# Two AV runs of two head pairs instead of four runs of one, and a full-array last block in the second GEMM

## The chip, the cores and the metric

The kernel runs on one core of a Trainium2 chip. The metric is the device time of the whole kernel in microseconds (us), from its first instruction to its last. Before the change it is 345.63 us, the median of three runs (345.2 to 345.86). The profile that is read below is one execution of its own, with a span of 343.4 us.

A core has five engines with a queue of instructions each: PE (TensorE, the matrix unit), DVE (VectorE), ACT (ScalarE), POOL (GpSimd) and SP (SyncE, which here only starts transfers). They wait for one another by semaphores.

## The reference

Forgetting attention for 8 batches of 8 heads, 576 tokens, head size 64, followed by a two-layer network with an exact GELU on all 4608 tokens:

```python
scores = scale * np.matmul(q, k.transpose(0, 1, 3, 2))
cum = np.cumsum(np.log(np.clip(f, 0.0001, 1.0)), axis=-1)
scores = np.where(causal, -1e9, scores + cum[:, :, :, None] - cum[:, :, None, :])
attn = softmax(scores)
x = np.matmul(attn, v)            # (8, 8, 576, 64), then to (4608, 512)
h = x @ w_in                      # 512 -> 2048
out = gelu(h) @ w_out             # 2048 -> 512
```

The kernel computes it in bfloat16 with sums in float32.

## The kernel before

**Attention.** The eight heads of a batch are four pairs (`i` = 0 to 3). Queries and keys are held transposed, one head of a pair in partitions 0 to 63 and the other in 64 to 127. For each pair, `scores` (L270) computes the causal part of the scores in four tiles (`t` = 0 to 3): keys in partitions, queries along the free axis, both heads side by side. Its matmuls contract over 64 rows, so they use half of the array's rows each, and the two heads run beside one another. The exponential on ACT (L299) brings a tile from PSUM to SBUF, and POOL zeroes what lies above the diagonal (L301). Score tiles live in two PSUM buffers of two banks ("s"), so a third tile can begin only when the exponential of the first is done.

`attend` (L313) multiplies the exponentials with the values, which carry the forgetting weights and a column for the softmax sum (this product is called AV). It is 15 matmuls of the full array, 128x65, for each head, into one PSUM bank; there are two such banks ("o"). `normalize` (L328) then takes the reciprocal of the sums (L333) and multiplies (L334), both on DVE, and writes x.

x must be transposed for the first GEMM. From the third batch on (`b` > 2) a transposing DMA on SP's queue does it for pairs 0 to 2 (`x_dma`, L358), and PE does it for pair 3 (`to_xT`, L346), through an "o" bank. In the batch `b` = 2 PE does it for pairs 2 and 3.

**First GEMM.** `gemm1` (L370) takes the first 512 tokens of the batch in 16 blocks of four full-array 128x512 matmuls, and GELU on ACT brings each block to SBUF. The last 64 tokens of all batches are gathered and done at the end.

**Second GEMM.** It is spread as filler into the attention of the next batch, so that PE has work while ACT computes exponentials. `gemm2_rows` (L446) is a generator of steps: four blocks of 128 tokens (`ts` = 0 to 3), 16 steps each, one for each 128 of the 2048 contracted elements. A step is written as "r" or "n". An "r" step is two half-array matmuls, rows 0 to 63 into one PSUM bank and rows 64 to 127 into another. An "n" step is one full-array matmul into the first bank. DVE copies the second bank out (L474) and adds the first (L476), and the block is stored from SP. A plan names for each block its number, the PSUM pool that it holds ("o", "m" or "s", of which "m" also serves the first GEMM), and its 16 steps. `take(fill, n)` (L521) issues the next n steps.

**The order of the work** is written out by hand; the engines run their instructions in that order. In `attention(b)` (L621), for `b` = 2 to 7, the sixteen score tiles are issued one after another, each followed by as many steps as `FILL` (for `b` = 2, `FILL_2`) says. After tile 1 of pairs 1, 2 and 3 come the two heads of AV of the pair before, and its `x_dma`. The AV of pair 3 follows the last score tile and eight more steps. Then come six steps, the transpose of pair 3, and the remaining steps. The batch `b` = 2 has more filler, `gemm2_third`: 16 full-array steps of `gemm2_half`, 32 steps of `PLAN_0` and 64 of `PLAN_1`.

Of the kernel before, what the change touches and what calls it, by code (L numbers as in the profile page):

```python
# [11 lines left out]
Alu = mybir.AluOpType  # L12
# [6 lines left out]
HP = 4  # L19
# [20 lines left out]
def where(n, m):  # L40

    q = K0[m]
    for t, parts in enumerate(STILES):
        c = 0
        for nn, q0, w in parts:
            if nn == n and q0 <= q and q + P <= q0 + w:
                return t, c + q - q0
            c += w
    raise KeyError((n, m))
# [3 lines left out]
def kernel(  # L53
# [10 lines left out]
    nc = tc.nc  # L64
# [5 lines left out]
    n_ff = d_ff // P  # L70
# [17 lines left out]
    s_psum = ctx.enter_context(tc.tile_pool(name="s_psum", bufs=2, space=PSUM))  # L88
    o_psum = ctx.enter_context(tc.tile_pool(name="o_psum", bufs=2, space=PSUM))
# [24 lines left out]
    def load_v(b, h0=0, h1=H):  # L114
        if b >= B:
            return
        for n in range(NBLK):
            p0 = D if n == NBLK - 1 else 0
            nc.sync.dma_start(
                v_sb[p0:P, h0:h1, n, :],  # L120
                v[b, h0:h1, K0[n] + p0 : K0[n] + P].rearrange("h p d -> p h d"),
            )
# [14 lines left out]
    for t, op, fill in (  # L137
# [7 lines left out]
            fill=fill,  # L145
# [74 lines left out]
    def transpose_dma(b, h0, h1):  # L220

        if b >= B:
            return
        if b not in tq_of:
            tq_of[b] = [
                tq_pool.tile([P, H, JT // 2, PT], BF16, tag="t" + n, name=f"t{n}{b}")
                for n in "qk"
            ]
        for src, dst in zip(qk_of[b], tq_of[b]):
            nc.sync.dma_start_transpose(  # L230
                dst[:, h0:h1].rearrange("d h j p -> d (h j) p"),
                src[:, h0:h1].rearrange("p h c -> p (h c)"),
            )
# [79 lines left out]
    def attend(b, i, h, ms):  # L313
        if (b, i, h) not in o_of:
            o_of[b, i, h] = o_psum.tile([P, NBLK, D + 1], FP32, tag="o", name="o")
        o = o_of[b, i, h]
        for m in ms:
            for n in range(m + 1):
                t, c = where(n, m)
                nc.tensor.matmul(  # L320
                    o[:, m, :],
                    e_of[b, i, t][:, h, c : c + P],
                    vw_of[b][:, 2 * i + h, n, :],
                    start=(n == 0),
                    stop=(n == m),
                )

    def normalize(b, i, h):  # L328
        if (b, i) not in x_of:
            x_of[b, i] = x_pool.tile([P, NBLK, 2, D], BF16, tag="x", name="x")  # L330
        o = o_of[b, i, h]
        r = x_pool.tile([P, NBLK], FP32, tag="r", name="r")
        nc.vector.reciprocal(r, o[:, :, D])  # L333
        nc.vector.tensor_tensor(  # L334
            x_of[b, i][:, :, h, :],
            o[:, :, 0:D],
            r.unsqueeze(2).to_broadcast([P, NBLK, D]),
            Alu.mult,
        )

    def xT(b):
        if b not in xT_of:
            xT_of[b] = xT_pool.tile([P, n_dm, XC], BF16, tag="xT", name="xT")
        return xT_of[b]

    def to_xT(b, i, copy, pool=m_psum, tag="m", ps=None):  # L346
        if ps is None:
            shape = [P, 2, 1024] if pool is s_psum else [P, XC]
            ps = pool.tile(shape, BF16, tag=tag, name="ps_x")
            if pool is s_psum:  # L350
                ps = ps[:, 0, 0:XC]
        for m in range(NBLK):
            nc.tensor.transpose(  # L353
                ps[:, m * P : (m + 1) * P], x_of[b, i][:, m, :, :], ident_bf
            )
        copy(xT(b)[:, i, :], ps)  # L356

    def x_dma(b, i):  # L358
        nc.sync.dma_start_transpose(
            xT(b)[:, i, :].rearrange("d (m p) -> d m p", p=P),  # L360
            x_of[b, i].rearrange("p m h d -> p (m h d)"),
        )

    def x_tail(b):
        nc.gpsimd.tensor_copy(tails[:, :, b * TL : (b + 1) * TL], xT(b)[:, :, XC - TL :])  # L365
# [28 lines left out]
    def gemm2(c):  # L394
# [35 lines left out]

    PLAN = [
        (0, "o", 16 * "r"),
        (1, "m", 6 * "r" + "n" + 8 * "r" + "n"),
        (2, "m", 9 * "r" + "n" + 6 * "r"),
        (3, "s", 7 * "r" + 9 * "n"),
    ]

    PLAN_0 = [(2, "o", 16 * "r"), (3, "m", 14 * "r" + 2 * "n")]
    PLAN_1 = [
        (0, "m", 14 * "r" + 2 * "n"),  # L440
        (1, "m", 14 * "r" + 2 * "n"),
        (2, "m", 14 * "r" + 2 * "n"),
        (3, "s", 8 * "r" + 8 * "n"),
    ]

    def gemm2_rows(c, plan):  # L446

        for ts, held, steps in plan:
            if held == "s":
                both = s_psum.tile([P, 2, d_model], FP32, tag="s", name="ps2")
                banks = [both[:, 0], both[:, 1]]
            else:
                pool = {"o": o_psum, "m": m_psum}[held]
                banks = [
                    pool.tile([P, d_model], FP32, tag=held, name="ps2")
                    for _ in range(2)
                ]  # L460
            ot = o_pool.tile([P, d_model], FP32, tag="ot", name="ot")
            for kt, step in enumerate(steps):
                last = kt == steps.rindex("r")
                for r in range(2 if step == "r" else 1):
                    rows = slice(r * D, (r + 1) * D) if step == "r" else slice(0, P)
                    nc.tensor.matmul(  # L466
                        banks[r],
                        g_of[c][kt][rows, ts * P : (ts + 1) * P],
                        w_out_sb[rows, kt, :],
                        start=kt == (steps.index("r") if r else 0),  # L470
                        stop=last if r else kt == n_ff - 1,
                    )
                if kt == n_ff - 1 if held == "s" else last:
                    nc.vector.tensor_copy(ot, banks[1])  # L474
                if kt == n_ff - 1:
                    nc.vector.tensor_tensor(ot, ot, banks[0], Alu.add)  # L476
                    store(c, ts, ot)
                yield

    def store(c, ts, ot):  # L480
        nc.sync.dma_start(out[c * S + ts * P : c * S + (ts + 1) * P, :], ot)
# [34 lines left out]
    def gemm2_third():  # L516
        yield from gemm2_half(0, 1)
        yield from gemm2_rows(0, PLAN_0)
        yield from gemm2_rows(1, PLAN_1)

    def take(gen, n):  # L521
        for _ in range(n):
            if next(gen, "end") == "end":
                return
# [89 lines left out]

    FILL = [[7, 6, 3, 3], [1, 3, 3, 2], [1, 3, 3, 3], [1, 3, 3, 3], [8]]
    FILL_2 = [[8, 8, 8, 8], [8, 8, 4, 4], [4, 4, 4, 4], [4, 4, 4, 4], [8]]
    FILL_1 = [[0, 0, 0, 0], [0, 0, 0, 0], [2, 2, 2, 2], [2, 2, 2, 2]]

    def attention(b):  # L621


        fill = gemm2_third() if b == 2 else gemm2_rows(b - 1, PLAN)
        counts = FILL_2 if b == 2 else FILL

        def av(i):
            for h in range(2):
                attend(b, i, h, (0, 1, 2, 3, 4))
                normalize(b, i, h)  # L630

        for i in range(HP):
            for t in range(4):
                scores(b, i, t)
                take(fill, counts[i][t])
                if i and t == 1:
                    av(i - 1)
                    if i < HP - 1 or b > 2:
                        x_dma(b, i - 1)
                if t == 1 and i == 0:  # L640
                    load_v(b + 1)
                if b > 2 and t == 0 and i < 2:
                    transpose_dma(b + 1, 4 * i, 4 * i + 4)
                if b == 2 and t == 1 and i == 1:
                    transpose_dma(3, 0, 4)
                    transpose_dma(3, 4, 8)
        take(fill, counts[HP][0])
        if b == 2:
            to_xT(b, HP - 2, nc.vector.tensor_copy, s_psum, "s")
        av(HP - 1)  # L650
        take(fill, 6)
        to_xT(b, HP - 1, nc.vector.tensor_copy, o_psum, "o")
        x_tail(b)
        take(fill, 999)
# [107 lines left out]
```

The softmax here doesn't subtract the row's maximum and nothing guards it: scores larger than these inputs give would overflow.

## Time and profile before

| | value |
|---|---|
| time | 345.63 us (345.2 to 345.86) |
| span of the profile | 343.4 us |
| from one batch to the next, `b` = 3 to 7 | 35.67 us |
| of it attention with the second GEMM (`b` = 4) | 21.77 us |
| of it the first GEMM | 13.9 us |
| one second-GEMM step, "r" or "n" | 0.216 us |
| AV of one head | 0.48 us |
| exponential of a tile of 128x896 | 0.917 us |
| copy and add of a second-GEMM block on DVE | 0.69 us each |

Busy time of PE is the time in which any of its matmuls is in the pipeline; matmuls overlap, so the rate of work is read from the distance of their starts, not from their lengths. In the chain of work that ended last, each piece is followed back to what released it, and a piece of PE there means that PE had nothing to wait for. A few records of matmuls are missing in the trace, which shows as a short gap with no releaser.

### The profile page before, as it was taken

Reading aid. Unit: us, or ns where it says so; the run is one execution under the profiler, and the core shown is the slowest. Engines: PE = TensorE matmul, PEld = TensorE weight load, DVE = VectorE, ACT = ScalarE, POOL = GpSimd, SP = SyncE. Lnnn points to the kernel's source line nnn. Section 1 sums busy time; section 2 is a strip of 40 time slices with the busy share of each in tenths; the row PEclk is TensorE's granted clock in tenths of the full one; section 3 lists DMA queues with packets and bytes.
Section 4 is the critical chain, followed back from the end, with each engine's and each line's share of the span. In section 5 each row is a group of like instructions: output and inputs, shape, how many; then the busy total and the mean of one; then the engine's idle time right before and its main releaser. Section 6 shows DMA issues by size and latency. Waiting matters only on the chain.

```text
span 343.4 us, 7895 instructions
## 1 busy us (share of the span) xinstructions
PE 328.6 (96%) x3182; PEld 174.7 (51%) x3227; DVE 187.0 (54%) x424; ACT 212.3 (62%) x296; POOL 124.2 (36%) x256
## 2 busy tenths in 40 slices
PE   7799999999999999999999999999999999999995
PEld 3574555445554456545654565446544654444443
DVE  5660355933467935796479646974597542020011
ACT  5986786773644787368746874687468755504600
POOL 8390672228328034543445243714261430000000
PEclk9999999999999999999999999999999999999999
DMA  8999999989993999578945896499900230011013
GB/s 117 178 176 194 201 166 153 170 158 148 237 184 102 139 192 188 82 101 165 211 121 73 141 212 139 71 160 198 169 31 2 65 88 31 2 61 61 0 38 87
DMA packets 99924, 43.03 MB, mean 125 GB/s; under 512 B 78704, under 2 KB 95344, under 8 KB 99888
## 3 DMA queue, kind: packets, MB, share of 16 engines
q1 hardware_dynamic: 82592, 28.37, 41.4%
q0 software_dynamic: 16896, 13.63, 27.2%
q8 instruction: 25, 0.41, 0.5%
q10 hardware_dynamic: 400, 0.52, 0.4%
q14 instruction: 11, 0.09, 0.1%
HBM read 36.85 MB, written 9.44 MB: 135 GB/s over the span
## 4 chain that ended last, share of the span: by engine, by line
PE 89%; issue 2%; POOL 2%; DVE 2%; ACT 2%; DMA 2%; POOLq 0%; ACTq 0%; DVEq 0%
PE ps L375 36%; PE ps L466 25%; PE o L320 9%; PE ps L408 8%; PE s L289 7%; PE ps L501 2%; ACT e L299 2%; DMA k<-in_k_dram 2%; PE ps_x L353 1%; DVE x L334 1%; POOL q L107 1%; PE ps_f L206 1%; POOL k L107 1%; DVE r L333 0%; DVE xT L356 0%
## 5 line engine op out<-in xcount | busy, mean ns | idle before, releaser
L392 ACT ACTIVATE g<-ps 128x512 bf16<-128x512 f32 x144 | 85.3, 597 | 81.1 <-PE ps L375 81.1
L299 ACT ACTIVATE e<-s 128x896 bf16<-128x896 f32 (+2 forms) x128 | 101.2, 836 | 28.5 <-PE s L289 26.8
L375 PE MATMUL ps<-xT,w_in_sb 128*128 128x512 bf16 x497 | 111.4, 379 | 0.8
L466 PE MATMUL ps<-w_out_sb,g 64*128 64x512 bf16 (+1 forms) x731 | 103.0, 376 | 0.8 <-issue 0.8
L375 PEld LDWEIGHTS <-w_in_sb 128*128 128x128 bf16 x576 | 56.0, 98 | 67.5 <-issue 1.8
L301 POOL TENSOR_SCALAR_AFFINE_SELECT e<-e 128x256 bf16<-128x256 bf16 (+1 forms) x135 | 49.2, 383 | 98.9 <-ACT e L299 98.6
L466 PEld LDWEIGHTS <-g 64*128 64x128 bf16 (+1 forms) x756 | 41.5, 94 | 40.4 <-issue 11.9
L244 DVE COPY qT<-tq 64x288 bf16<-64x288 bf16 x96 | 48.7, 507 | 1.4
L289 PE MATMUL s<-qT,kT 64*128 64x320 bf16 (+4 forms) x384 | 45.8, 276 | 3.6 <-ACT e L299 2.7
L260 POOL TENSOR_TENSOR vw<-v_sb,wT 128x640 bf16<-128x640 f32 x31 | 39.6, 1278 | 23.5 <-DMA v_sb<-in_v_dram 23.3
L320 PE MATMUL o<-vw,e 128*128 128x65 bf16 x960 | 36.8, 194 | 3.5 <-issue 2.4
L474 DVE COPY ot<-ps 128x512 f32<-128x512 f32 x26 | 17.9, 689 | 37.1 <-PE ps L466 35.2
L320 PEld LDWEIGHTS <-e 128*128 128x128 bf16 x960 | 34.8, 98 | 5.3 <-PE ps_x L353 0.3
L244 DVE COPY kT<-tk 64x288 bf16<-64x288 bf16 x96 | 33.0, 343 | 1.6
L334 DVE TENSOR_TENSOR x<-o,r 128x320 bf16<-128x320 f32 x64 | 31.4, 491 | 2.4 <-DVE r L333 0.2
L417 DVE COPY ot<-ps 128x512 f32<-128x512 f32 (+2 forms) x9 | 5.7, 632 | 48.8 <-PE ps L408 31.9
L289 PEld LDWEIGHTS <-kT 64*128 64x128 bf16 x384 | 19.5, 94 | 23.2 <-issue 9.7
L408 PE MATMUL ps<-w_out_sb,g 128*128 128x512 bf16 (+2 forms) x142 | 27.9, 355 | 0.1
L333 DVE RECIPROCAL r<-o 128x5 f32<-128x5 f32 x64 | 12.1, 189 | 27.6 <-PE o L320 27.5
L408 PEld LDWEIGHTS <-g 128*128 128x128 bf16 x144 | 13.5, 98 | 14.5
L476 DVE TENSOR_TENSOR ot<-ot,ps 128x512 f32<-128x512 f32 x26 | 17.9, 687 | 1.5
L365 POOL COPY tails<-xT 128x256 bf16<-128x256 bf16 x8 | 3.2, 399 | 31.3 <-DVE xT L356 31.3
(64 smaller groups left out, 158.1 us busy)
## 6 DMA issues: line engine op xcount, KB each, us to landing
out_dram<-ot SPq DMA_DIRECT2D x32, 256.0 KB, 2.3
v_sb<-in_v_dram SPq DMA_DIRECT2D x24, 256.0 KB, 5.3
q<-in_q_dram POOLq DMA_DIRECT2D x6, 576.0 KB, 6.1
k<-in_k_dram POOLq DMA_DIRECT2D x6, 576.0 KB, 8.2
v_sb<-in_v_dram SPq DMA_DIRECT2D x22, 128.0 KB, 5.1
w_in_sb<-in_moe_w_in_dram POOLq DMA_DIRECT2D x4, 512.0 KB, 6.7
w_out_sb<-in_moe_w_out_dram POOLq DMA_DIRECT2D x4, 512.0 KB, 8.4
q<-in_q_dram POOLq DMA_DIRECT2D x4, 144.0 KB, 4.6
```

The source lines that it names most:

```text
L244: nc.vector.tensor_copy(rows[:, odd], src[odd * D : (odd + 1) * D, 2 * i + h].rearrange("d j p -> d p j"),)
L260: eng.tensor_tensor(vw_of[b][:, hs, :, 0:D], v_sb[:, hs, :, :], w.unsqueeze(3).to_broadcast([P, 2, NBLK, D]), Alu.mult,)
L289: nc.tensor.matmul(to, *ab, start=half < 0, stop=half == 1 or not masked)
L299: nc.scalar.activation(et[:, :, z:c], st[:, :, z:c], Act.Exp, scale=scale)
L301: nc.gpsimd.affine_select(out=et[:, :, c0 + z : c0 + P], in_=et[:, :, c0 + z : c0 + P], compare_op=Alu.is_ge, fill=0.0, base=z, pattern=[[ ...
L320: nc.tensor.matmul(o[:, m, :], e_of[b, i, t][:, h, c : c + P], vw_of[b][:, 2 * i + h, n, :], start=(n == 0), stop=(n == m),)
L334: nc.vector.tensor_tensor(x_of[b, i][:, :, h, :], o[:, :, 0:D], r.unsqueeze(2).to_broadcast([P, NBLK, D]), Alu.mult,)
L375: nc.tensor.matmul(ps, w_in_sb[:, kt, ffb * P : (ffb + 1) * P], src[:, kt, 0:TC], start=(kt == 0), stop=(kt == n_dm - 1),)
L392: nc.scalar.activation(g_of[c][ffb], ps, Act.Gelu)
L408: nc.tensor.matmul(pss[ts][:, c0:c1], g_of[c][kt][:, ts * P : (ts + 1) * P], w_out_sb[:, kt, c0:c1], start=(kt == 0), stop=(kt == n_ff - 1),)
L466: nc.tensor.matmul(banks[r], g_of[c][kt][rows, ts * P : (ts + 1) * P], w_out_sb[rows, kt, :], start=kt == (steps.index("r") if r else 0), ...
L474: nc.vector.tensor_copy(ot, banks[1])
```

## The change

Four edits belong together, all of them in work of the batches `b` = 2 to 7.

1. AV: the runs after tile 1 of pairs 1 and 3 are dropped. After tile 1 of pair 2 the four heads of pairs 0 and 1 are issued, with one second-GEMM step behind each of the first two. The four heads of pairs 2 and 3 follow the last score tile, with three steps after the second head and one after the third.
2. Plans: the last block (`ts` = 3) is 16 "n" steps, with one copy on DVE in place of a copy and an add. The other blocks become "r" throughout, but for two "n" steps in block 1, which fall between the AV heads. In `PLAN_1` block 1 holds the "o" banks in place of "m".
3. `FILL` and `FILL_2`: the counts are set to the new order, and the eight steps ahead of pair 3's AV are gone.
4. The transposing DMA of pair 0 is issued after the run of pair 2, together with pair 1's; pair 2's comes after its AV in the tail. In `b` = 2 the PE transpose of pair 2 goes through an "o" bank in place of a score buffer and comes after pair 3's AV.

```diff
     PLAN = [
         (0, "o", 16 * "r"),
-        (1, "m", 6 * "r" + "n" + 8 * "r" + "n"),
-        (2, "m", 9 * "r" + "n" + 6 * "r"),
-        (3, "s", 7 * "r" + 9 * "n"),
+        (1, "m", 14 * "r" + 2 * "n"),
+        (2, "m", 16 * "r"),
+        (3, "s", 16 * "n"),
     ]
...
     PLAN_1 = [
-        (0, "m", 14 * "r" + 2 * "n"),
-        (1, "m", 14 * "r" + 2 * "n"),
-        (2, "m", 14 * "r" + 2 * "n"),
-        (3, "s", 8 * "r" + 8 * "n"),
+        (0, "m", 16 * "r"),
+        (1, "o", 16 * "r"),
+        (2, "m", 16 * "r"),
+        (3, "s", 16 * "n"),
     ]
...
-                if kt == n_ff - 1 if held == "s" else last:
+                if last:
                     nc.vector.tensor_copy(ot, banks[1])
                 if kt == n_ff - 1:
-                    nc.vector.tensor_tensor(ot, ot, banks[0], Alu.add)
+                    if "r" in steps:
+                        nc.vector.tensor_tensor(ot, ot, banks[0], Alu.add)
+                    else:
+                        nc.vector.tensor_copy(ot, banks[0])
                     store(c, ts, ot)
...
-    FILL = [[7, 6, 3, 3], [1, 3, 3, 2], [1, 3, 3, 3], [1, 3, 3, 3], [8]]
-    FILL_2 = [[8, 8, 8, 8], [8, 8, 4, 4], [4, 4, 4, 4], [4, 4, 4, 4], [8]]
+    FILL = [[7, 6, 3, 3], [1, 3, 3, 2], [1, 1, 3, 3], [1, 3, 3, 3]]
+    FILL_2 = [[8, 8, 5, 5], [4, 4, 4, 4], [2, 2, 6, 6], [9, 9, 9, 9]]
...
-        def av(i):
-            for h in range(2):
-                attend(b, i, h, (0, 1, 2, 3, 4))
-                normalize(b, i, h)
+        def av(i, h, n=0):
+            attend(b, i, h, (0, 1, 2, 3, 4))
+            normalize(b, i, h)
+            take(fill, n)
...
-                if i and t == 1:
-                    av(i - 1)
-                    if i < HP - 1 or b > 2:
-                        x_dma(b, i - 1)
+                if (i, t) == (2, 1):
+                    av(0, 0, 1)
+                    av(0, 1, 1)
+                    x_dma(b, 0)
+                    av(1, 0)
+                    av(1, 1)
+                    x_dma(b, 1)
...
-        take(fill, counts[HP][0])
+        av(HP - 2, 0)
+        av(HP - 2, 1, 3)
+        if b > 2:
+            x_dma(b, HP - 2)
+        av(HP - 1, 0, 1)
+        av(HP - 1, 1)
         if b == 2:
-            to_xT(b, HP - 2, nc.vector.tensor_copy, s_psum, "s")
-        av(HP - 1)
+            to_xT(b, HP - 2, nc.vector.tensor_copy, o_psum, "o")
         take(fill, 6)
         to_xT(b, HP - 1, nc.vector.tensor_copy, o_psum, "o")
```

More of the change, by code (lines that the diff above doesn't have):

```diff
@@ L462, in gemm2_rows @@
             for kt, step in enumerate(steps):
-                last = kt == steps.rindex("r")
+                last = kt == steps.rfind("r")
                 for r in range(2 if step == "r" else 1):
```

## The prediction

> **What bounds the kernel now.** I read four views in this order: the page for the engine that carries the span, busy time by stretch for the stages, the chain of waits inside one batch for the joints between kinds of matmul, and the timeline for what the other engines do at those joints. The page:
>
> ```profile
> PE 328.6 (96%) x3182; PEld 174.7 (51%) x3227; DVE 187.0 (54%) x424; ACT 212.3 (62%) x296; POOL 124.2 (36%) x256
> PE 89%; issue 2%; POOL 2%; DVE 2%; ACT 2%; DMA 2%; POOLq 0%; ACTq 0%; DVEq 0%
> ```
>
> TensorE (PE) is busy for 96% and is 89% of the chain that ended last. So a change counts by what it does to PE's starts. Next, two stretches of the fifth batch (b = 4): its attention and the first GEMM behind it. The columns are length, then busy us (and instructions) of PE, weight loads, VectorE (DVE), ScalarE (ACT), GpSimd, then clock, DMA share and GB/s.
>
> ```profile
> 155.08:176.85 21.77, 21.12 (x287) 12.59 (x291) 11.88 (x31) 15.73 (x19) 7.29 (x20) 1.00 0.95 179
> 176.85:190.40 13.55, 13.45 (x62) 6.17 (x63) 13.13 (x27) 8.76 (x15) 7.86 (x11) 1.00 0.53 89
> ```
>
> Attention takes 21.77 us and PE leaves little of it idle; ACT has 6 us free and DVE 10, so they can only hurt in places. GEMM 1 is PE back to back and the change does not touch it. The chain inside this attention (start, us, what):
>
> ```profile
> 159.88 0.36 PE L289 MATMUL s<-qT,kT 64*128 64x256 bf16 x4
> ...
> 160.45 0.60 PE L466 MATMUL ps<-w_out_sb,g 64*128 64x512 bf16 x4
> 161.21 1.11 PE L320 MATMUL o<-vw,e 128*128 128x65 bf16 x30 [0.16 <-issue]
> 162.25 0.36 PE L289 MATMUL s<-qT,kT 64*128 64x448 bf16 x2
> ...
> 164.28 0.34 PE L289 MATMUL s<-qT,kT 64*128 64x64 bf16 x4
> ```
> ```profile
> 164.28 0.34 PE s L289 x4
> 164.62 0.43 PE ps L466 x4
> 165.05 0.16 issue
> 165.21 1.11 PE o L320 x30
> 166.32 0.29 PE s L289 x2
> ...
> 171.57 2.16 PE ps L466 x20
> 173.73 0.16 issue
> 173.89 1.11 PE o L320 x30
> ```
>
> The first block is the PE timeline, the second the chain. An AV run is 30 full-array matmuls; it stands between half-array (64-row) score and GEMM 2 matmuls. One GEMM 2 step is 0.216 us, whether it is "r" or "n" (20 matmuls, 10 "r" steps, in 2.16). The "0.16 issue" hides one "n" step whose record is missing. Price of a joint: the last "r" before the first AV starts at 160.67 (end 161.05, one lasts 0.376); AV starts at 161.21, 0.54 later, of which "r" and "n" are 0.43. So 64 to 128 rows costs **0.10 us**. Back: the last AV matmul starts at 162.13, the score tile at 162.25; 0.13 less 0.032 (AV spacing, 30 in 0.95) again leaves **0.10 us**. 164.28 with 0.34 us is a score tile that waited 0.17 us for ACT to free its PSUM buffer.
>
> What DVE does just ahead of the last AV:
>
> ```profile
> 172.26 0.69 DVE L474 COPY ot<-ps 128x512 f32<-128x512 f32 x1 [0.86 <-PE ps L466]
> 172.99 0.69 DVE L476 TENSOR_TENSOR ot<-ot,ps 128x512 f32<-128x512 f32 x1
> 174.56 0.20 DVE L333 RECIPROCAL r<-o 128x5 f32<-128x5 f32 x1 [0.89 <-PE o L320]
> ```
>
> The third token block's copy and add (1.41 us) are over at 173.68, before the normalisation wants DVE: eight fill steps stand between. The first batch shows AV heads without such steps:
>
> ```profile
> 22.34 0.49 DVE x L334
> 22.83 0.11 DVE r L333
> 22.95 0.03 issue
> 22.98 0.63 PE o L320 x15
> ```
>
> There are two "o" banks, so head n waits for the normalisation of head n-2. Here PE starts 0.146 us after that multiply ends at 22.836; the plain DVE to PE waits elsewhere take 0.055.
>
> **What the Trainium skill says.** "TensorEngine Tiling (Array Packing)", section Key Properties: changing the tiling mode drains TensorE. The trace agrees: 0.10 us each way. "TensorE: Matmul & The Clock Gate", section Architectural detail: only weight loads are pulled ahead, and VectorE and ScalarE are strict FIFO. The trace agrees: a waiting score tile holds all matmuls behind it, and the first batch's normalisation stands behind a copy issued earlier. "PSUM — Partial Sum Buffer", section Terms: a matmul output lies in one bank, and two engines on one bank at once is an error, so an AV run cannot start in a bank that DVE reads. "Perfetto Trace Analysis", section Identifying Dependency Chains: several waits of one instruction can become separate instructions ahead of it; this is such a place in the trace (the 0.146 us) and is my upper price.
>
> **The change part by part (one batch, b = 3 to 7).** I lay the new order against the times of b = 4, queue by queue, with the durations above: exp 0.917, 0.806, 0.917, 0.70 us for the four tiles, back-to-back exps overlapping by 0.1; exp end to next score 0.05; score start to exp 0.40 to 0.49; one AV head 0.476; normalisation 0.72 (0.19 + 0.49 + gaps), 0.63 when queued behind another. The same working on the old order puts GEMM 1 at 176.80 (trace 176.85) and finds its waits: 0.02 and 0.19 at two score tiles (trace 0.015, 0.17), and 0.12 at a GEMM 2 bank (trace 0.17).
>
> *Removed: mode changes.* Old: AV after pairs 0, 1, 2 (six), into the tail, back to scores: 8. New: in and out once, tail, back: 4. Gain 4 x 0.10 = **-0.40**. Steps (64), scores and AV are as many as before.
>
> *Less PE work between scores.* From (1,1) to (2,1) the old order has AV of pair 0 (1.15 us with its switches) to let ACT catch up. The new one has six tiles with 11 steps in a row; ACT needs 3.34 us for four tiles, PE only about 3.3. Tile (1,2) is ready at 161.10 but exp (1,0) ends 161.27: 0.22. Then (2,0) waits 0.12 and (2,1), with one step before it, 0.19. After the AV run, AV of pair 2 is missing behind (3,1): tile (3,2) is ready at 169.47, exp (3,0) ends 169.64: 0.22. Sum **+0.75**; the old 0.19 goes.
>
> *Four heads in a row.* AV (0,0) starts at 163.93. DVE's queue: copy of block 1 (to 164.73), normalise (0,0) (to 165.37), (0,1) (to 165.99), add of block 1 (to 166.68), then pair 1. AV (1,0) is ready at 165.32 and starts at 165.42; (1,1) is ready at 165.90 and starts at 166.05: **+0.26**. Block 2 then finds its bank free: the old bank wait (0.17) goes.
>
> *The tail.* The last "r" of block 2 now stands directly ahead of AV of pair 2: step at 171.10, AV (2,0) 171.41, (2,1) 171.89, three "n" to 173.01. DVE: copy 171.52 to 172.21, add to 172.93, normalise (2,0) only then, to 173.56, since it was issued behind them; (2,1) to 174.19. AV (3,0) needs the bank of (2,0): 173.62 instead of 173.01, **+0.61**. AV (3,1) is ready after one more step at 174.31, its bank at 174.25: no wait. Queued behind it: all of the tail and GEMM 1. Normalise (3,1) ends at 175.65 and the transposes come at 176.1: hidden behind six "n".
>
> *Moved DMA.* The transposing DMA of pair 2 goes from 172.1 to 174.3, when its x is written, behind block 2's store on SP's queue; issue 1.24 us, landing 2.6 to 2.8 us after its start (largest of all 4.9): 177.0. GEMM 1's third matmul wants it at 178.1: free. Those of pairs 0 and 1 start when SP is done with loads (168.1 either way). *Last block all "n":* same 0.216 a step, one DVE op of 0.69 fewer, beside GEMM 1: nothing.
>
> Sum: +0.75 +0.26 +0.61 -0.40 -0.35 (old waits) = **+0.87**. With 0.146 instead of 0.055 at two of the bank waits +1.05. I take 0.95: five batches **+4.75**.
>
> *Batch 2* has 15 switches inside and 7 after: -0.80, and 0.09 of an old wait goes. It has steps in plenty (four to nine a tile), so no exp waits. Bank waits as above, 0.26 and 0.61, plus the transposes of pair 2, which now take an "o" bank instead of a score buffer and wait for normalise (3,0): 0.23. Net +0.2 to +0.5; I take **+0.3**.
>
> Total +5.05. The profiled span of 343.4 would become 348.4; the timed runs (345.2 to 345.86) stand 2.2 above the span, and I keep that: 345.63 + 5.05 = **350.7**.
>
> **Rivals.** *Faster: the switch is dearer than its gap shows*, for instance because loads run late for several steps behind it. Place: 28 removed switches (5 x 4 + 8). New waits less old ones are 5 x 1.27 + 1.0 = 7.4 us, so it decides from 0.26 us a switch; at 0.36 the time is about 343. Against it: step spacing behind every AV is 0.216 from the second step on. *Half of it:* the tail's normalisation does not hold AV (3,0), if the wait there is shorter than queue order makes it. Then 6 x 0.61 falls away: 347.0. Against it: DVE runs in program order throughout. *Late transpose:* pair 2's DMA takes the 4.9 us seen at worst, 1.05 us beyond its slack, in five batches: 355.9. For it: only 3.8 us now lie between its start and its reader, and a store goes ahead of it. Against it: pair 2's landed in 2.6 us in this batch, with the same store behind it.
>
> **How the numbers follow.** Likeliest 0.77 (349.5 to 352.2), half 0.10, late transpose 0.06, faster 0.07. The range 346.9 to 352.6 holds the first two cases less their tails. Runs of before spread by 0.2%, so that is what can be told from no change: faster 0.08, same 0.03, slower 0.89, the "same" being the lower tail of the half case.
>
> **What would show it.** AV runs of 60 and two AV stretches a batch; PE waiting for DVE's multiply ahead of AV (3,0) by about 0.6 us and of (1,0), (1,1) by 0.1 to 0.2; score tiles (1,2), (2,0), (2,1), (3,2) waiting for exp, 0.1 to 0.2 each; attention of 22.7 us instead of 21.8, GEMM 1 unchanged at 13.9 (176.85 to the next score tile at 190.75). Wrong if those AV heads start without idle time, if the batch period falls below 35.66, or if GEMM 1's third matmul waits for a DMA.

## The result and the profile after

The changed kernel takes 351.08 us (median of four runs, 350.52 to 351.89) against 345.75 for the kernel before in the same comparison: a ratio of 1.0155, with a 95% interval of 1.0126 to 1.0183. It is slower by 5.3 us; 350.7 was forecast. The profiled span went from 343.4 to 349.1 us, 5.6 more. Single executions lie 2 to 4 us above their kernel's median, most of them with a lower granted clock (the kernel before once took 350.07 us at a clock of 0.993, against a median of 345.87), so medians are compared here.

The page of the changed kernel, busy time and the chain of work that ended last:

```profile
PE 335.4 (96%) x3195; PEld 175.0 (50%) x3195; DVE 183.4 (53%) x418; ACT 210.6 (60%) x296; POOL 124.7 (36%) x256
PE 64%; DMA 10%; SPq 7%; DVE 6%; ACT 5%; POOL 4%; issue 2%; ACTq 0%; POOLq 0%; DVEq 0%
```

PE is busy for the same share of a longer span. What changed is the chain: PE fell from 89% to 64% of it, and DVE and ACT, 2% each before, now hold 11% together. (DMA and SP have a large share because the chain leaves PE in batch 2 and goes back through a late transfer, of which more below; a share of the chain is not a loss of the same size.) The two stretches of the fifth batch, attention and first GEMM, in the same columns as before:

```profile
156.45:179.14 22.69, 22.02 (x284) 12.65 (x284) 11.59 (x30) 15.41 (x19) 7.76 (x22) 1.00 0.89 165
179.14:193.05 13.91, 13.91 (x65) 6.14 (x64) 13.25 (x28) 8.96 (x15) 7.39 (x10) 1.00 0.62 101
```

Attention has grown from 21.76 to 22.70 us, in all five batches alike; the first GEMM is as long as it was. The chain in that attention (start, us, what; pieces under 0.05 us are left out) shows where:

```profile
161.40 0.21 PE s L289 x4
161.72 0.93 ACT e L299
162.68 0.37 PE s L289 x2
...
165.39 0.62 DVE ot L474
166.00 0.19 DVE r L333
166.21 0.49 DVE x L334
166.71 0.16 DVE r L333
166.87 1.21 PE o L320 x30
...
172.93 0.70 DVE ot L474
173.65 0.69 DVE ot L477
174.34 0.12 DVE r L333
174.48 0.49 DVE x L334
174.97 0.11 DVE r L333
175.12 0.63 PE o L320 x15
```

Read from the top: a score tile (1,2) starts only when an exponential on ACT ends; the second half of the merged AV run starts behind block 1's copy and a normalisation; and in the tail the third AV head starts behind block 2's copy, its add and a normalisation, one after another on DVE. (The last DVE piece ahead of each AV is the reciprocal of the head after; what frees the bank is the multiply before it. It ends at 166.71 and 174.97, and both times PE starts 0.146 us later, with a wait instruction of its own, of 0.05 us, in PE's queue: the same as in the first batch.) A piece of PE in the chain can hide a short wait: the last two heads of the merged run take 1.21 us there because the fourth waits 0.11 us. The timeline of PE across the tail says what that costs:

```profile
172.82 1.12 PE L320 MATMUL o<-vw,e 128*128 128x65 bf16 x30
173.78 0.81 PE L466 MATMUL ps<-w_out_sb,g 128*128 128x512 bf16 x3
175.12 0.63 PE L320 MATMUL o<-vw,e 128*128 128x65 bf16 x15 [0.52 <-DVE r L333]
175.59 0.38 PE L466 MATMUL ps<-w_out_sb,g 128*128 128x512 bf16 x1
```

The three full-array steps start at 173.78, so AV head (3,0) could start 3 x 0.216 later, at 174.43. It starts at 175.12: 0.69 us are lost. (The bracket says 0.52 because it counts from the end of the last step's matmul, which stays in the pipeline for 0.38 us, and not from when the next matmul could have been started.)

The changed kernel's times in batch 4, by the starts of PE's instructions, against the forecast: score tiles (1,2), (2,0), (2,1), (3,2) waited 0.22, 0.09, 0.17, 0.22 us (0.22, 0.12, 0.19, 0.22); AV heads (1,0) and (1,1) 0.18 and 0.11 (0.10 and 0.16); AV head (3,0) 0.69 (0.61, and 0.70 at the upper price). Together 1.68 us. Less four mode changes (0.40) and the old waits (0.35) this is 0.93 us a batch; the batch grew by 0.94.

The span's other parts: batch 2's attention took 33.47 us instead of 33.00 (+0.47), the start before batch 2 came out 0.05 shorter, and in the last batch this stretch of the chain appears:

```profile
285.45 4.38 DMA xT<-x
289.82 0.04 issue
289.87 13.54 PE ps L375 x62
```

The transposing DMA of pair 2 took 4.4 us to land, and the first GEMM's third matmul waited 0.47 us for it. The sum is 5 x 0.94 + 0.47 + 0.47 - 0.05 = 5.6, the whole difference of the spans.

### The profile page after: what moved, and what is told of

It reads as the page before. It is cut to its first block, busy times and chain, and to the rows that moved or that the text cites. A ratio compares the mean times of both kernels' runs of the same rounds, so it can differ in the third digit from the quotient of the medians.

```text
span 349.1 us, 7871 instructions
## 1 busy us (share of the span) xinstructions
PE 335.4 (96%) x3195; PEld 175.0 (50%) x3195; DVE 183.4 (53%) x418; ACT 210.6 (60%) x296; POOL 124.7 (36%) x256
## 4 chain that ended last, share of the span: by engine, by line
PE 64%; DMA 10%; SPq 7%; DVE 6%; ACT 5%; POOL 4%; issue 2%; ACTq 0%; POOLq 0%; DVEq 0%
PE ps L375 31%; PE ps L466 14%; PE ps L408 8%; PE s L289 5%; ACT e L299 4%; DMA v_sb<-in_v_dram 4%; PE o L320 4%; SPq L119 3%; DMA k<-in_k_dram 3%; SPq L230 3%; DMA xT<-x 2%; DVE x L334 2%; DVE ot L474 2%; POOL vw L260 1%; POOL q L107 1%
## 5 line engine op out<-in xcount | busy, mean ns | idle before, releaser
L299 ACT ACTIVATE e<-s 128x896 bf16<-128x896 f32 (+2 forms) x128 | 99.5, 838 | 26.8 <-PE s L289 24.3
L375 PE MATMUL ps<-xT,w_in_sb 128*128 128x512 bf16 x512 | 112.7, 379 | 0.3 <-DMA xT<-x 0.3
L466 PE MATMUL ps<-w_out_sb,g 64*128 64x512 bf16 (+1 forms) x724 | 110.6, 376 | 0.0
L466 PEld LDWEIGHTS <-g 64*128 64x128 bf16 (+1 forms) x724 | 40.5, 95 | 29.2
L244 DVE COPY qT<-tq 64x288 bf16<-64x288 bf16 x96 | 49.6, 517 | 1.5
L289 PE MATMUL s<-qT,kT 64*128 64x320 bf16 (+4 forms) x384 | 44.1, 276 | 4.0 <-ACT e L299 2.7
L474 DVE COPY ot<-ps 128x512 f32<-128x512 f32 x20 | 13.8, 691 | 60.3 <-PE ps L466 60.3
L320 PE MATMUL o<-vw,e 128*128 128x65 bf16 x960 | 39.5, 194 | 3.5 <-DVE r L333 3.1
L289 PEld LDWEIGHTS <-kT 64*128 64x128 bf16 x384 | 20.3, 94 | 28.3 <-issue 13.6
L375 PE MATMUL ps<-tails,w_in_sb 128*128 128x512 bf16 x64 | 14.3, 377 | 0.0
```

Source lines behind the costliest of these rows:

```text
L244: nc.vector.tensor_copy(rows[:, odd], src[odd * D : (odd + 1) * D, 2 * i + h].rearrange("d j p -> d p j"),)
L289: nc.tensor.matmul(to, *ab, start=half < 0, stop=half == 1 or not masked)
L299: nc.scalar.activation(et[:, :, z:c], st[:, :, z:c], Act.Exp, scale=scale)
L320: nc.tensor.matmul(o[:, m, :], e_of[b, i, t][:, h, c : c + P], vw_of[b][:, 2 * i + h, n, :], start=(n == 0), stop=(n == m),)
L375: nc.tensor.matmul(ps, w_in_sb[:, kt, ffb * P : (ffb + 1) * P], src[:, kt, 0:TC], start=(kt == 0), stop=(kt == n_dm - 1),)
L466: nc.tensor.matmul(banks[r], g_of[c][kt][rows, ts * P : (ts + 1) * P], w_out_sb[rows, kt, :], start=kt == (steps.index("r") if r else 0), ...
```

## The experiments

The theory is the prediction's: a mode change costs 0.10 us, and the merged runs pay more than they save, because score tiles come to wait for ACT and AV heads for DVE. The rivals are that the mode change costs something else, that the full-array last block carries the loss, that PE's waits are not for what the trace names, and that the late transpose is the cause.

### What a mode change costs

```diff
 (kernel before)
-        (3, "s", 7 * "r" + 9 * "n"),
+        (3, "s", "rnrnrnr" + 9 * "n"),
```

> The kernel before with three of the seven half-array steps of the last block (rnrnrnr and then nine n), so that PE changes between 64 and 128 rows six times more in each of five batches; the work is the same. Own theory (a switch costs 0.10 us): 30 x 0.10 = 3.0 us slower than before, about 348.7. Rival (a switch costs 0.26 us or more and the change loses elsewhere): 7.8 us slower or more, above 353. If switches are free: no change.

Measured: 348.94 us against 345.87, a ratio of 1.0087 (1.0063 to 1.0112): 3.07 us for 30 mode changes, **0.102 us each**. Every attention of batches 3 to 7 grew from 21.76 to 22.40 us, 0.64 for six. The gap read off the trace was the whole price. The rival that needed 0.26 us falls, and with it the idea that the 28 switches which the change takes away could be worth more than 28 x 0.102 = 2.9 us.

### The full-array last block alone

```diff
 (kernel before)
-        (3, "s", 7 * "r" + 9 * "n"),
+        (3, "s", 16 * "n"),
 # and one copy in place of copy and add for a block without "r"
```

> The kernel before with its last block of batches 3 to 7 as 16 full-array steps and one copy, AV runs left where they were. The number of mode changes stays the same, a step costs 0.216 us either way, and the DVE operation saved lies beside the first GEMM. Own theory: no change (within 0.7 us). Rival (the full-array block itself carries the loss): about 5 us slower.

Measured: 345.91 us against 345.87, ratio 0.9996 (0.9974 to 1.0018). This part of the change costs nothing and brings nothing, though it takes a DVE operation out of each batch. So the loss lies in the rest of the change: the order of the AV runs and the steps around them.

### The wait of the third tail head

```diff
 (changed kernel)
+        take(fill, 5)
         av(HP - 2, 0)
         av(HP - 2, 1, 3)
 ...
-        take(fill, 6)
+        take(fill, 4)
```

> The changed kernel with five of the last block's steps moved ahead of the tail's AV run, so that DVE can copy and add block 2 while PE works. Own theory: the wait of AV head (3,0), 0.69 us in each of six batches, goes, but where pair 2's transposing DMA lands late (batch 7, 4.4 us in the changed kernel) it takes part of it back: 3 to 4 us faster than the changed kernel, 347 to 348. Rival (PE waits there for something else, or the wait moves to the first GEMM in every batch): within 1 us of the changed kernel.

The time was 349.37 us (ratio 1.0086, 1.0059 to 1.0114): 1.7 us below the changed kernel's first runs, half of what was expected. The wait itself went as the theory has it. PE's timeline in the tail of this kernel:

```profile
172.63 1.11 PE L320 MATMUL o<-vw,e 128*128 128x65 bf16 x30
173.58 0.81 PE L466 MATMUL ps<-w_out_sb,g 128*128 128x512 bf16 x3
174.23 0.64 PE L320 MATMUL o<-vw,e 128*128 128x65 bf16 x15
174.70 0.38 PE L466 MATMUL ps<-w_out_sb,g 128*128 128x512 bf16 x1
```

The third head starts 0.65 us after the first of the three steps, with no bracket: nothing was waited for. Attention fell from 22.70 to 22.14 us in each of the five batches, and the profiled span by 3.3 us to 345.8. The attention gives back 0.56 of the 0.69 us: with four steps instead of six ahead of them, the transposes of pair 3 now start at 176.37 instead of 176.25, since they wait for that pair's normalisation. The fall of the span is as expected; the median of the runs is not. In the profile one batch waits 0.79 us in the first GEMM for pair 2's DMA. Two kernels were run for the gap between span and median. First the changed kernel again, on the chip of the next runs:

> The changed kernel as it is, on the same chip as the three beside it, because the kernel with five steps ahead of the tail's AV run came out 1.7 us below the changed kernel's 351.1 where its profiled span had come down by 3.3. Own theory (the runs vary with the landing of pair 2's transposing DMA, and the first four runs were typical): 350.5 to 351.5. Rival (the changed kernel's first runs were high by chance): 350.5 or below.

351.21 us (350.7 to 351.38): the changed kernel's first runs were typical. Then the kernel above, without that DMA:

```diff
 (kernel above)
         av(HP - 2, 1, 3)
-        if b > 2:
-            x_dma(b, HP - 2)
         av(HP - 1, 0, 1)
         av(HP - 1, 1)
-        if b == 2:
-            to_xT(b, HP - 2, nc.vector.tensor_copy, o_psum, "o")
-        take(fill, 4)
+        take(fill, 2)
+        to_xT(b, HP - 2, nc.vector.tensor_copy, o_psum, "o")
+        take(fill, 2)
```

> The kernel with five steps ahead of the tail's AV run, and with pair 2 transposed by PE in batches 3 to 7 instead of by DMA: 0.28 us more of PE in each of five batches, 1.4 us, and no wait for that DMA in any batch. Own theory (late landings of this DMA are what made that kernel's runs 1.1 us slower in the median than its profiled run): its median stays within 1 us of the profiled run, at 348 to 349, and its runs scatter less than 348.2 to 353.0. Rival (the scatter has another source): 1.4 us above that kernel's 349.4, 350.8, with the same scatter.

347.68 us (347.2 to 348.58; ratio 1.006, 1.0039 to 1.0081), below the range expected (348 to 349), though PE does five transposes more in each of five batches. Its attentions are 22.29 us long, 0.15 more than with the DMA, and batch 2's 32.30. From these, 5 x 0.53 - 0.70 = 1.95 us above before is to be expected, and 2.0 was measured. The kernel with the DMA was run once more on another chip:

> The kernel with five steps ahead of the tail's AV run once more, on another chip. By its stage times (attention 0.38 us longer than before in five batches, batch 2 0.08 longer, one late DMA of 0.8) it should be 2.8 us slower than before, 348.5. Own theory: that holds, or the median is higher by late landings of pair 2's DMA in more than one batch, 348.5 to 349.5. Rival (the earlier 349.4 was that chip's scatter): 348.0 to 348.5.

349.05 us (348.57 to 350.81). In this execution two batches waited for the DMA in the first GEMM, 0.25 and 0.87 us. So moving the steps ahead of the tail's AV takes 2.8 us out of the five attentions (5 x 0.56), and a part comes back because the later DMA no longer has room for a slow landing. That the untraced runs were held up in the same way, and more often, is argued from the faster kernel without the DMA, not seen.

### The wait of the score tiles

```diff
 (changed kernel)
-        nc.scalar.activation(et[:, :, z:c], st[:, :, z:c], Act.Exp, scale=scale)
+        c1 = z + (c - z) // 2 if b > 2 and i else c
+        nc.scalar.activation(et[:, :, z:c1], st[:, :, z:c1], Act.Exp, scale=scale)
 # and 16 fixed buffers for the exponentials in place of the pool
```

> The changed kernel with the exponentials of pairs 1 to 3 in batches 3 to 7 over half their columns only; the other half keeps the values of the batch before (part of the work is left out). The exponentials lie in fixed buffers instead of a pool of as many. Own theory: the four score tiles that wait for ACT, 0.70 us a batch in the changed kernel's trace, no longer do: attention 22.0 us instead of 22.7, 3.5 us faster than the changed kernel. Rival (these tiles are held by something else, or the wait moves to the AV heads behind them): less than 1 us.

Measured: 347.68 us (347.34 to 348.68), 3.53 below the changed kernel's 351.21 on the same chip. The chain through the same place no longer holds ACT (line numbers have moved by three or four):

```profile
162.76 0.17 PE s L292 x4
162.93 0.65 PE ps L470 x6
163.57 0.19 PE s L292 x2
163.76 0.65 PE ps L470 x6
164.41 0.14 PE s L292 x2
```

Tile (1,2) follows its steps at 163.57 without a gap. Attention is 21.93 us, 0.77 less, where 0.70 was expected. DVE's pieces ahead of the merged run's second half and of the third tail head stay in this kernel's chain, as they should: the two kinds of wait are separate and add up.

### The wait of pair 1's heads

```diff
 (changed kernel; PLAN_0's last block likewise)
-        (1, "m", 14 * "r" + 2 * "n"),
+        (1, "m", 13 * "r" + 3 * "n"),
 ...
-                    av(0, 1, 1)
+                    av(0, 1, 2)
 # FILL and FILL_2: one step fewer behind tile (2, 1)
```

> The changed kernel with one more full-array step between the second and the third AV head of the merged run (block 1 as 13 r and 3 n; one step fewer ahead of the run). Own theory: the two heads of pair 1 wait 0.18 and 0.11 us for DVE in the changed kernel's trace; the step fills most of it: 0.2 to 0.25 us less in each of six batches, attention 22.45 to 22.5 us, 1.2 to 1.5 us faster than the changed kernel. Rival (the gaps there are the price of full-array heads in a row and not a wait for the bank): no change.

Attention is 22.48 us in all five batches, 0.22 less, as the theory has it: the step between the heads took the place of the wait. The time does not settle it: 351.48 us, but with runs from 349.68 to 352.84 (ratio 1.0155, 1.01 to 1.0211), too wide for 1.1 us. In its profiled execution batch 2 took 33.90 us, 0.4 more than in the changed kernel's, although that batch has the same change to its heads; how much batch 2 varies by itself is told below, at the end of the experiments.

### A version with the waits taken out

```diff
 (changed kernel)
-        (1, "m", 14 * "r" + 2 * "n"),
-        (2, "m", 16 * "r"),
+        (1, "m", 13 * "r" + 3 * "n"),
+        (2, "m", 9 * "r" + "n" + 6 * "r"),
 ...
-    FILL = [[7, 6, 3, 3], [1, 3, 3, 2], [1, 1, 3, 3], [1, 3, 3, 3]]
-    FILL_2 = [[8, 8, 5, 5], [4, 4, 4, 4], [2, 2, 6, 6], [9, 9, 9, 9]]
+    FILL = [[7, 6, 2, 3], [2, 4, 2, 3], [0, 2, 3, 3], [1, 1, 3, 3]]
+    FILL_2 = [[8, 8, 5, 5], [4, 4, 4, 4], [3, 8, 8, 8], [8, 8, 4, 4]]
 ...
-                if (i, t) == (2, 1):
+                if (i, t) == (2, 0):
                     av(0, 0, 1)
-                    av(0, 1, 1)
+                    av(0, 1, 2)
 ...
+                if (i, t) == (3, 1):
+                    av(2, 0)
+                    av(2, 1)
+                    if b > 2:
+                        x_dma(b, 2)
 # PLAN_0's last block: 13 r and 3 n
 # tail: eight steps, (b == 2: transpose of pair 2), pair 3's AV, six steps, as before
```

> A version that keeps one merged run, of pairs 0 and 1, one tile earlier (behind tile 0 of pair 2), with one full-array step between its first heads and two ahead of the third, pair 2's AV alone behind tile 1 of pair 3 as before, eight steps ahead of pair 3's AV as before, and the steps spread so that ACT keeps up. By the queue working of the prediction its waits are 0.2 us a batch; attention 21.4 us instead of 21.76 (before) and 22.70 (after); batch 2 has 9 mode changes inside instead of 15. Own theory: 5 x 0.36 + 0.5 = 2.3 us faster than the kernel before, 343.5. Rival (a merged run costs more than its waits show): no faster than before.

Measured: **343.39 us** against 345.68, ratio 0.9941 (0.9917 to 0.9965): 2.3 us faster than the kernel before, and 7.8 faster than the changed one. Attention is 21.38 us in four of the five batches. The chain of one of them at the merged run:

```profile
165.39 0.22 PE s L289 x4
165.61 0.58 PE o L320 x15
166.19 0.22 PE ps L466
166.41 0.47 PE o L320 x15
166.88 0.43 PE ps L466 x2
167.31 1.02 PE o L320 x30
168.34 0.27 PE s L289 x4
```

Nothing but PE stands in it: four heads with three steps among them, one way in and one way out. Only the fourth head still waits, 0.07 us, inside the piece of 1.02 us. What the merging is worth can be estimated from the price of a mode change: two fewer in each of five batches and six fewer in batch 2 are 16 x 0.10 = 1.6 of the 2.3 us. In the five batches the attention is 0.38 us shorter, 0.20 of it for the mode changes; the other 0.18 must come from the waits of the kernel before (0.36 us), of which, by difference, half are gone. So one merged run pays where steps fill the time that DVE needs between heads and ACT has had its share first. A kernel with four separate AV runs and its steps placed as well as here was not run, so the parts are an estimate.

In batch 3 of that profiled execution attention took 22.28 us, since pair 3's normalisation waited for pair 0's DMA (4.6 us to land) to free one of three x buffers. With four buffers:

> The faster version with four instead of three buffers for x. In its profiled run batch 3 took 22.28 us instead of 21.38, because the normalisation of pair 3 waited for the transposing DMA of pair 0 to let go of the buffer. Own theory: that wait goes in all batches; every attention of batches 3 to 7 takes 21.4 us, median 342.7 to 343.4, less scatter than 342.7 to 347.6. Rival (that DMA is waited for by the first GEMM anyway): no change.

All five attentions are 21.38 us now, so that wait was real; but the median is 343.85 us, above the range expected, and on this chip 1.6 us below the kernel before (ratio 0.9954, 0.9935 to 0.9974). The two intervals overlap: the fourth buffer shows no gain. The same in the changed kernel, one execution:

> The changed kernel with four instead of three buffers for x, one look. Own theory: in batch 2 the normalisation of head (3,0) no longer waits for the DMA of pair 0 (0.22 us in the changed kernel's trace), so batch 2's attention takes 33.2 us instead of 33.47; batches 3 to 7 stay at 22.70. Rival (the wait there is SP's backlog and moves to the first GEMM): 33.4 or more, or a gap in the first GEMM.

Batch 2 took 33.53 us, not 33.2: a miss. The normalisation of head (3,0) follows its reciprocal without the wait, at 102.04, but the time does not show. Batch 2 varies by itself: its attention took 33.47 and 33.62 us in two executions of the same changed kernel, and 33.92 in the kernel with the full-array last block alone, whose batch 2 is that of the kernel before, against 33.00 there (its chain goes back to a late load of the values). A term of 0.2 can't be seen against 0.9.

## Why the prediction was right

*Mode changes, -0.40 us a batch.* Right; 0.10 us by the trace, 0.102 by the run with 30 more.

*Score tiles, +0.75.* Right: 0.70 in the trace, and 0.77 when the exponentials were shortened. Laying ACT's and PE's queues side by side named all four tiles, two of them 0.02 to 0.03 us too long. These tile-by-tile times carry the term; the round comparison beside them, 3.34 us on ACT for four tiles against about 3.3 on PE, does not, since it leaves out that exponentials overlap. In the trace after, four exponentials take 2.97 us there, from the start of the first at 161.72 to that of the fifth at 164.68, and PE needs 2.67 us from tile (1,1) to tile (2,1) when its waits are taken off.

*Four heads in a row, +0.26.* Right in size (0.29), and the step of mid-run filler that removed 0.22 shows the cause. Its two parts were shared out otherwise, because the first head waited at the upper of the two prices for a wait on DVE.

*Tail, +0.61.* Right, at the upper price: 0.69.

*Moved DMA, free.* Wrong in one batch of five. The step gave it a landing of 2.6 to 2.8 us and 1.1 us of room. In the last batch it took 4.4 us, and 0.47 us showed (0.23 in another execution of the same kernel). One of the prediction's own signs of being wrong, the first GEMM's third matmul waiting for a DMA, came true in one batch. The rival of a late transpose was the right mechanism, but for one batch, not for five. The trace of before already held the sign: pair 2's DMA took 4.1 us in its last batch and 4.9 in batch 3, where nothing waited for it. The prediction names the 4.9 as the worst, but takes the landing of one batch for the normal one in all. The DMA of pair 0, which was to start at 168.1 either way, in fact started later: 14.56 us after the start of its batch's attention instead of 13.16 (b = 4). Nothing waited for it there.

*Last block, nothing.* Right; its run alone gave no change.

*Batch 2, +0.3.* 0.47 in the traces that were compared, but against a scatter of up to 0.9 us in that batch, so that the term is neither confirmed nor refuted. One wait was missing from it: the x buffer that pair 3's normalisation waits for (0.22 us), since pair 0's DMA is issued later there. The run with four buffers could not size what it costs.

In sum +5.05 was forecast, against +5.6 in the spans and +5.3 in the medians; in the spans the two terms that were short are the DMA (0.47) and batch 2 (0.17).

*One reading that does not hold in full.* The prediction holds that only weight loads are pulled ahead in PE's queue. Between the two row halves of the array the trace of before shows something else, and the measurement decides:

```profile
167.10 0.30 PE L289 MATMUL s<-qT,kT 64*128 64x320 bf16 x1
167.24 0.38 PE L466 MATMUL ps<-w_out_sb,g 64*128 64x512 bf16 x1
167.27 0.29 PE L289 MATMUL s<-qT,kT 64*128 64x320 bf16 x1
```

The two score matmuls stand ahead of the step in the program, one for each half. The first half's step starts at 167.24, before the second half's score matmul at 167.27. The forecast does not hang on it, since a score tile that waits for ACT waits at its first matmul, and all that follows it waits too.

## What to carry to other kernels

Before runs of one kind are merged to save mode changes, price the change from the gap at one joint, and then lay out what the split runs did for others: here each AV run gave ACT time to catch up, and each gap between runs gave DVE time to empty a bank. A consumer that needs 0.63 to 0.72 us a piece and has two buffers paces a producer of 0.48 us pieces from the third piece on; other work put between the pieces costs nothing, the same work put elsewhere leaves a wait. A long operation that is issued just ahead of the one that frees a buffer (copy and add, 1.41 us) is paid by whoever waits for that buffer, less the work that lies between (here three steps, 0.65 us, which left 0.69 us of waiting).

## What was not expected of the hardware

The transposing DMA of one 128x640 bf16 tile has no fixed time to landing: pair 2's takes 2.6 us in most batches and 2.9 to 4.9 in some. The traces show what goes with the long ones. Each block has lines of the DMA view of the changed kernel from issue to landing (queue, packets, MB, share; then the DMA and its landing in us), first in the fifth batch, then in the last:

```profile
q1 hardware_dynamic: 736, 0.26, 42.0%
xT<-x SPq DMA_TRANSPOSE x1, 2.6
```
```profile
q1 hardware_dynamic: 735, 0.26, 77.6%
q8 instruction: 1, 0.02, 1.3%
xT<-x SPq DMA_TRANSPOSE x1, 4.4
```

The two moved the same in 735 and 736 packets, but for one packet of 16 KB on a queue that the profile names "instruction". Twelve traces of this case have this DMA in batches 3 to 7, 60 times. In 37 of them no packet of an instruction queue was in flight during the first 2.4 us: all landed in 2.55 to 2.66 us. In the other 23 one was: 22 took 2.94 to 4.88 us, one 2.57. In the last batch one was in flight in all seven executions of the changed kernel and of its variants that keep this DMA behind the tail's first two heads (landings of 3.56 to 4.38 us), so the late landing there is no accident. That the packet causes the delay is not shown, since no run moved it.

Two half-array matmuls of 64x512 that follow one another into two banks start within 0.01 us of each other and, pair by pair, 0.216 us apart, exactly as one full-array matmul does. Where one of the two had to wait for its bank or its score buffer, the halves stayed 0.02 to 0.17 us apart over several steps and closed up again later, so waits of the two halves can lie beside one another, and a wait of one half is not always a wait of PE.
